# One small load moved from ScalarE's queue to GpSimd's, and one pair of warm-up matmuls taken out, in the start-up of a fused attention and FFN kernel

## The chip, the cores and the metric

The kernel runs on one core of a Trainium2 chip. The metric is the device time of one execution in microseconds (us), lower is better. Times here are of fast runs; row_alone and before_again are single runs, whose state is unknown. The span in a profile is 1.2 to 1.3 us shorter than the device time, since it starts with the first instruction of the program and ends with the last.

TensorE (PE) has two rows in a profile: PE for matmuls and PEld for the loads of their stationary operand. VectorE is DVE, ScalarE is ACT, GpSimd is POOL, and SyncE is SP. SP and ACT issue the transfers (DMAs) here, and in the changed kernel POOL issues one of them.

## The reference

Two branches over the same tokens are mixed by a gate: a linear attention and a SwiGLU FFN.

```python
x = A_x                                               # 1 x 2048 x 640, bf16
g = _sigmoid((x * gate_w).sum(-1, keepdims=True))     # one gate per token
a = _A_ref(x, wqkv, w_phi, wo)                        # 32 heads of 20, softmax feature maps
b = _B_ref(x, w_gate, w_up, w_down)                   # hidden size 1728
return g * a + (1 - g) * b
```

## The kernel before

One long list, `ORDER`, says in which order PE works; loads are issued in front of it in the order of `LOADS`. Only the first few microseconds matter here. There, x comes in 128-token tiles x0 to x3, the v columns of `wqkv` in five row blocks w0 to w4, and the gate vector as a row of 640 numbers, which PE turns into a 641st column beside them. So the gate's dot product comes out of the same matmuls as v.

```python
LOADS = """ x0 w0 x1 w1 x2 w2 x3 w3 w4 f0 h ... """
ORDER = """
H0 ... H9 X0 G H10 H11 H12 U0.0 X1 H13 U1.0 U0.1 X2 U1.1 U2.0 U0.2 ... """

XQ = ["sp", "act", "act", "act"]          # queues of x0..x3
WQ = ["sp", "sp", "sp", "sp", "act"]      # queues of w0..w4
dma("act", gwr[0:5, :], ...gate_w...)     # the gate row, in front of all other ACT loads

def gcol():        # G: turn the gate row, copy it into column 640 of wvg
    ...
    transposes([(o, gwr[0:5, :])], 5)
    copy("dve", wvg[:, :, D:D + 1], o.unsqueeze(2))

def warm():        # H: NWARM = 2 matmuls of constants, their result is not used
    ...
def load_phi():    # h: ACT waits for w3, then loads w_phi
    tr._wait("act", dict([wv_evs[3]]))
    dma("act", wph[:, :, :], ...)
def kv_end():      # N
    for _ in range(NPEW):                 # NPEW = 16
        pe.wait_ge(tr.sem["pe"], 1)       # always met already
```

`X0` turns x0 (five transposes on PE, two copies on DVE), `U0.0` is the first v part (x0 times w0, two matmuls of 320 and 321 columns), `M1` much later needs `w_phi`. The H matmuls keep PE busy while it waits for data.

The softmax here doesn't subtract the row's maximum and nothing guards it: scores larger than these inputs give would overflow.

## Time and profile before

| | before |
|---|---|
| device time, median of 5 runs | 288.73 us (288.59 to 289.27) |
| span in the profile | 287.60 us |
| PE busy | 99% |
| x0, w0, x1 landed | 3.08, 3.89, 4.30 us |
| gate row issued by ACT, landed | 0.82, 2.17 us |
| first v part starts | 4.50 us |
| last matmul at the slow pitch starts | 5.47 us |

The prediction below shows the main lines. One view is added: the timeline of PE alone, just after the start-up. Columns are start, duration, engine, line, operation, what is written and read, shape, and count.

```profile
5.71 0.71 PE L296 MATMUL ps<-wvg,xT 128*128 128x320 bf16 x4
...
6.54 1.53 PE L296 MATMUL ps<-wvg,xT 128*128 128x320 bf16 x10
...
8.19 3.46 PE L296 MATMUL ps<-wvg,xT 128*128 128x320 bf16 x24
11.49 0.38 PE L296 MATMUL ps<-xT,wg 128*128 128x512 bf16 x1
```

Ten matmuls of 320 and 321 columns in 1.53 us is the full pitch, 0.136 us from start to start. Before 5.6 us the same matmul takes 0.267 us. The trace's record of the granted clock begins at 5.61 us, with full clock. Below, "half clock" and "slow pitch" both mean the pitch of 0.267 us for 320 columns (0.107 us for 128, against 0.056 us later). The first FFN matmul (`wg`), at 11.49 us, is a good mark for the end of the start-up.

### The profile page before, as it was taken

How to read it: one execution, taken by the hardware profiler on the slowest of the kernel's cores; microseconds unless marked ns; L12 is line 12 of the kernel's file. 1: busy time of each engine (PE TensorE's matmuls, PEld its weight loads, DVE VectorE, ACT ScalarE, POOL GpSimd, SP SyncE). 2: the span in 40 equal slices, each digit the busy share in tenths (PEclk: the TensorE clock that was granted, in tenths of full speed). 3: DMA queues.
4: the chain of work that ended last, by engine and by line, in shares of the span. 5: the costliest groups of instructions: out<-in, count | busy, mean ns of one | idle time of the engine just before them, and what ended most of it. 6: DMA issues, size and time to landing. Idle time of an engine off the chain costs nothing.

```text
span 287.6 us, 4959 instructions
## 1 busy us (share of the span) xinstructions
PE 284.9 (99%) x1977; PEld 175.2 (61%) x1977; DVE 163.4 (57%) x243; ACT 151.8 (53%) x252; POOL 159.8 (56%) x125
## 2 busy tenths in 40 slices
PE   8999999999999999999999999999999999999997
PEld 7667777675644545557775556675554446656776
DVE  2237748576469978689991465970317899100000
ACT  0767778676775565683535653225576552234112
POOL 8286999879446789836543438350753558501000
PEclk9999999999999999999999999999999999999999
DMA  7979488000010598202393002061020006210101
GB/s 219 190 133 123 100 251 317 5 1 2 2 47 0 114 297 162 51 2 50 65 158 70 5 1 50 2 149 42 2 50 0 3 1 123 52 46 0 49 23 48
DMA packets 48944, 21.62 MB, mean 75 GB/s; under 512 B 39384, under 2 KB 48792, under 8 KB 48920
## 3 DMA queue, kind: packets, MB, share of 16 engines
q1 hardware_dynamic: 47534, 20.59, 32.0%
q10 hardware_dynamic: 1386, 0.71, 0.9%
q8 instruction: 16, 0.26, 0.4%
q14 instruction: 8, 0.07, 0.1%
HBM read 9.29 MB, written 2.62 MB: 41 GB/s over the span
## 4 chain that ended last, share of the span: by engine, by line
PE 99%; DVE 0%; issue 0%
PE ps L296 97%; PE ps L477 1%; PE ps L308 1%; DVE osb L732 0%
## 5 line engine op out<-in xcount | busy, mean ns | idle before, releaser
L324 POOL TENSOR_TENSOR hT<-hT,us 128x512 bf16<-128x512 bf16 (+1 forms) x56 | 65.0, 1173 | 65.3 <-DVE hT L328 47.0
L328 DVE SCALAR_TENSOR_TENSOR hT<-hT,ps 128x512 bf16<-128x512 bf16 (+1 forms) x56 | 37.4, 683 | 66.9 <-ACT hT L314 53.3
L296 PE MATMUL ps<-xT,wg 128*128 128x512 bf16 x260 | 64.6, 379 | 0.0
L296 PE MATMUL ps<-xT,wu 128*128 128x512 bf16 x260 | 64.6, 379 | 0.0
L296 PE MATMUL ps<-wd,hT 128*128 128x320 bf16 (+2 forms) x462 | 63.9, 295 | 0.0
L324 POOL TENSOR_TENSOR ph<-eq,qc 128x1320 bf16<-128x1320 bf16 x16 | 42.3, 2644 | 25.6 <-DVE qc L637 22.2
L296 PEld LDWEIGHTS ps<-wd,hT 128*128 128x128 bf16 x462 | 44.5, 98 | 17.4
L296 PE MATMUL ps<-wqk,xT 128*128 128x320 bf16 x320 | 47.7, 299 | 0.0
L314 ACT ACTIVATE hT<-ps 128x512 bf16<-128x512 f32 (+2 forms) x60 | 35.8, 596 | 16.7 <-PE ps L296 16.5
L296 PEld LDWEIGHTS ps<-xT,wu 128*128 128x128 bf16 x260 | 25.5, 98 | 30.6
L314 ACT ACTIVATE us<-ps 128x512 bf16<-128x512 f32 (+1 forms) x56 | 33.5, 598 | 19.2 <-PE ps L296 18.2
L314 ACT ACTIVATE osb<-ps,omg 128x640 bf16<-128x640 f32 (+2 forms) x17 | 12.9, 757 | 55.8 <-PE ps L296 55.8
L296 PEld LDWEIGHTS ps<-xT,wg 128*128 128x128 bf16 x260 | 25.1, 98 | 27.8 <-ACT oT L314 0.8
L324 POOL TENSOR_TENSOR ekr<-ekr,krec 128x1280 bf16<-128x1280 bf16 x16 | 37.4, 2357 | 5.8 <-DVE krec L338 5.8
L296 PEld LDWEIGHTS ps<-wqk,xT 128*128 128x128 bf16 x320 | 30.5, 98 | 13.1 <-issue 0.4
L314 ACT ACTIVATE eq<-ps 128x640 bf16<-128x640 f32 x32 | 22.3, 703 | 20.9 <-POOL ph L324 10.7
L335 DVE TENSOR_REDUCE ksum<-ekr 128x64 f32<-128x1280 bf16 x16 | 23.5, 1470 | 11.7 <-ACT ekr L314 11.7
L314 ACT ACTIVATE ekr<-ps 128x640 bf16<-128x640 f32 x32 | 22.3, 703 | 8.7 <-PE ps L296 8.2
L335 DVE TENSOR_REDUCE qz<-eq 128x64 f32<-128x1280 bf16 x16 | 23.7, 1478 | 2.6 <-ACT eq L314 2.6
L296 PE MATMUL ps<-wog,oT 128*128 128x320 bf16 (+2 forms) x165 | 24.7, 294 | 0.0
L296 PE MATMUL ps<-wvg,xT 128*128 128x320 bf16 (+1 forms) x160 | 24.6, 301 | 0.0
L335 DVE TENSOR_REDUCE qw<-ez 128x64 f32<-128x1280 bf16 x16 | 23.6, 1476 | 0.0
(73 smaller groups left out, 190.4 us busy)
## 6 DMA issues: line engine op xcount, KB each, us to landing
out_dram<-osb SPq DMA_DIRECT2D x15, 160.0 KB, 1.9
wd<-in_B_w_down_dram SPq DMA_DIRECT2D x1, 2080.0 KB, 10.7
wg<-in_B_w_gate_dram SPq DMA_DIRECT2D x1, 1040.0 KB, 10.1
wu<-in_B_w_up_dram SPq DMA_DIRECT2D x1, 1040.0 KB, 12.2
wg<-in_B_w_gate_dram SPq DMA_DIRECT2D x1, 800.0 KB, 6.2
wu<-in_B_w_up_dram SPq DMA_DIRECT2D x1, 800.0 KB, 7.8
wog<-in_A_wo_dram SPq DMA_DIRECT2D x2, 375.0 KB, 7.2
wvg<-in_A_wqkv_dram SPq DMA_DIRECT2D x4, 160.0 KB, 4.2
```

Of the source, the lines that this page charges most:

```text
L296: last = pe.matmul(o, lhsT=l, rhs=r, start=st, stop=sp_, skip_group_check=sk)
L308: last = pe.transpose(o, i, ident[0:k, 0:k])
L314: return run("act", lambda: act.activation(o, i, func, scale=scale), rd, [o])
L324: return run(e, lambda: eo.tensor_tensor(o, a, b, op), [a, b], [o])
L328: return run("dve", lambda: dve.scalar_tensor_tensor(out=o, in0=a, scalar=s, in1=b, op0=op0, op1=op1), rd, [o])
L335: return run("dve", lambda: dve.tensor_reduce(o, i, AX.X, ALU.add), [i], [o])
L477: last = pe.matmul(bank(2 * pr, 0, P), lhsT=c, rhs=c, start=True, stop=True)
```

## The change

The intent: ACT's queue opens with x1 in place of the small gate row, so x1 comes sooner; GpSimd, which has nothing to load, takes the row. One pair of warm-up matmuls in front of the first v part is dropped. The added waits lie at the end of the k phase.

```diff
-NPEW = 16
+NPEW = 24
@@ ORDER
-H0 ... H9 X0 G H10 H11 H12 U0.0 X1 H13 U1.0 ...
+H0 ... H9 X0 G H10 H11 U0.0 X1 H12 U1.0 ...
@@
-    dma("act", gwr[0:5, :], bass.AP(gate_w.tensor, gate_w.offset, [[P, 5], [1, P]]))
+    dma("pool", gwr[0:5, :], bass.AP(gate_w.tensor, gate_w.offset, [[P, 5], [1, P]]))
```

More of the change, by code (lines that the diff above doesn't have):

```diff
@@ L38 @@
 ORDER = """
-H0 H1 H2 H3 H4 H5 H6 H7 H8 H9 X0 G H10 H11 H12 U0.0 X1 H13 U1.0 U0.1 X2 U1.1 U2.0 U0.2 U1.2 U2.1
+H0 H1 H2 H3 H4 H5 H6 H7 H8 H9 X0 G H10 H11 U0.0 X1 H12 U1.0 U0.1 X2 U1.1 U2.0 U0.2 U1.2 U2.1
 X3 U2.2 U0.3 U1.3 U2.3 U0.4 U1.4 U2.4 V3 Y F0.1 M1 i3 M0 F0.0 M2 V4 M3 M4 K0 K1 I S0 V6 V5 S1 P0
```

## The prediction

> **What bounds the kernel now.** I read the page's busy shares first, then the chain that ended last, then the first 14 us of the timeline, where everything that the change touches lies, and last the DMA landings there.
>
> The busy line and the chain say that this is one long TensorE program:
>
> ```profile
> PE 284.9 (99%) x1977; PEld 175.2 (61%) x1977; DVE 163.4 (57%) x243; ACT 151.8 (53%) x252; POOL 159.8 (56%) x125
> ...
> PE 99%; DVE 0%; issue 0%
> PE ps L296 97%; PE ps L477 1%; PE ps L308 1%; DVE osb L732 0%
> ```
>
> A busy PE is not proof of a full PE, since matmul ends are modelled. I therefore compared the start-to-start times of all matmuls after 5.7 us with columns / 2.4 + 2.5 ns. They fit (0.136 us for 320 columns, 0.216 us for 512) everywhere but at twelve places around the matmuls that read phiT, 0.83 us in all, none touched here. So nothing on VectorE, ScalarE, GpSimd or the queues delays PE from 5.7 us to the end. The end is "when the start-up is over" plus a constant. L477 are the dummy matmuls, L308 the transposes, L296 the real work.
>
> The start-up, from the timeline:
>
> ```profile
> 0.80 0.20 POOL L342 MEMSET ident<- 128x128 bf16 x1 [0.29 <-POOLq L791]
> 0.80 0.40 SPq L350 DMA_DIRECT2D xs<-in_A_x_dram  x1
> ...
> 0.82 0.56 ACTq L350 DMA_DIRECT2D gwr<-in_gate_w_dram  x1
> ...
> 1.24 0.29 POOL L356 TENSOR_SCALAR_AFFINE_SELECT ident<-ident 128x128 bf16<-128x128 bf16 x1 [0.23 <-POOL ident L342]
> ...
> 1.41 1.32 ACTq L350 DMA_DIRECT2D xs<-in_A_x_dram  x3
> ...
> 3.12 0.45 PEld L308 LDWEIGHTS ps<-ident,xs 128*128 128x128 bf16 x5 [0.26 <-DMA xs<-in_A_x_dram]
> ...
> 3.77 0.10 PEld L308 LDWEIGHTS ps<-ident,gwr 5*128 5x128 bf16 x1 [0.20 <-issue]
> ...
> 3.89 0.82 PE L477 MATMUL ps<-const-bfloat16-1.0 128*128 128x128 bf16 x6
> ...
> 4.22 0.17 DVE L320 COPY wvg<-ps 128x5 bf16<-128x5 bf16 x1
> 4.45 0.21 PEld L296 LDWEIGHTS ps<-wvg,xT 128*128 128x128 bf16 x2
> 4.50 0.74 PE L296 MATMUL ps<-wvg,xT 128*128 128x320 bf16 x2
> 4.77 0.74 PEld L308 LDWEIGHTS ps<-ident,xs 128*128 128x128 bf16 x5
> ```
>
> PE waits for x0 (3.12), turns it, turns the gate row (3.77), runs six dummies, then the first v part. That part waits for VectorE's copy of the gate column, which ends at 4.39. Its weight load starts 0.05 us later, and its matmul another 0.05 us later, when the last dummy leaves the array. Only this last 0.05 us is the dummies' doing. The issues in the same stretch are worth a second look:
>
> ```profile
> wvg<-in_A_wqkv_dram SPq DMA_DIRECT2D x4, 160.0 KB, 4.2
> xs<-in_A_x_dram ACTq DMA_DIRECT2D x3, 160.0 KB, 3.9
> ...
> xs<-in_A_x_dram SPq DMA_DIRECT2D x1, 160.0 KB, 2.3
> ```
>
> Adding each issue's landing time to its start: x0 3.08, w0 3.89, x1 4.30, w1 5.50, x2 5.68, w2 6.85, x3 7.05, w3 7.48, w4 7.83 (wN are the row blocks of wvg). PE's weight loads that wait on them start at 3.12, 4.45 (by way of VectorE), 4.77, 5.85, 6.12, 6.95, 7.77, 8.33, 9.16. So x0 has no slack, w2 has 0.10 us, w1 0.35 us, x1 0.47 us. The thing that the change hurries, x1, is not what PE waits for now.
>
> [...] In the trace's packet records the gate row's first packet starts 0.94 us after its ACT issue and it lands 1.35 us after[...]. No GpSimd DMA exists before. [...] from 3.1 to 7.8 us one 160 KB block lands per 0.6 us, whichever queue sent it. [...] Here the pitch of 128-column matmuls is 107 ns until the clock record turns to full at 5.61 us, then 56 ns. [...] Sixteen such blocks are in queue q8, and no PE gap lies near one.
>
> **The change part by part.**
> 1. Two dummies fewer before the first v part: 2 x 0.107 = 0.21 us of cold PE work, of which 0.16 us would only become waiting for VectorE. The matmul can start at 4.45 in place of 4.50: gain 0.05 us. The three-item order after it keeps one dummy pair behind x1. x1's turn, its copies on VectorE and the next v part all follow the first v part, so the 0.05 us is carried.
> 2. The gate row through GpSimd: PE needs it at 3.77 (and loses nothing until about 3.9, as VectorE is busy to 4.22). [...]
> 3. ACT's queue opens with x1 at 0.82 in place of 1.41. Gain by itself: none (slack 0.47). But it crowds others. In the packet records w0's packets follow x0's at about 2.5 us and x1's only begin at 2.98, as if blocks were served in the order of issue. Now x1 stands beside x0 and ahead of w0, and each later x block moves up one place as well. If x0 is slowed, the whole start-up slips. If the places merely swap, x1 lands near 3.9, w0 near 4.3 to 4.4 (need 4.39), w1 near 5.7 (need 5.85), w2 near 7.05 (need 6.95, less what PE gained). The last costs 0.1 to 0.15 us. w3 late by 0.35 us would also put off w_phi, which ACT issues after it, and the M1 matmuls that need it (weight load at 13.43, GpSimd's product done at 13.19): again 0.1 to 0.15 us, but the same delay, not a second one.
> 4. Eight more waits at the end of the k phase. The trace has them two to a record, 106 ns apart: 4 x 0.106 = 0.42 us of PE's sequencer near 75.5 us, while the sequencer is over 1 us ahead of the array (wait for VectorE done at 76.5, matmul at 77.6). Nothing.
>
> Sum for the middle case: -0.05 + 0.12, or +0.07 us: 288.8 us.
>
> **The rivals.** (a) *The hand-over helps*: blocks swap without harm to x0 and w2, only the dummies count: -0.05 us, 288.68. For it: the engines are far from full at 5.2 to 6.4 us in the packet records, so there is room. (b) *x1 slows x0*: if their packets alternate on the 16 engines, x0 lands 0.1 to 0.4 us later. [...] up to +0.3 us: 289.0. For it: the gate row's packets (1.76) came beside x0's (1.84), so two queues are not strictly in line. Against: x1's were not. (c) *The gate row is late*: if GpSimd's path needs over 3.1 us, the column, and with it all, slips by the excess; over 1 us is unlikely. (d) *The clock*: PE idles 0.16 us more before 5.6[...].
>
> **Range and chances.** I give (a) 3 in 10, the swap with a small loss 3 in 10, (b) and (c) together 3 in 10, the rest to (d) and the unknown. The three runs before spread over 0.28 us, so I widen to 288.4 to 289.3. A 2% change is 5.8 us[...]. Within 2%: 0.985.
>
> **What would show it.** Right: the first v part's load still 0.05 us after the gate column's copy; gate row landing before 3.7; x1 landing well before 4.3 and w2 after 6.85; PE without gaps after the start-up; end shifted by just what M1 is shifted. Wrong: x0's turn later than 3.2 (rival b), the gate row's turn waiting for a DMA (c), the 56 ns pitch setting in at a quite different time (d), or a new gap near 77.6 us (the waits do count).

The sum for the middle case: -0.05 us of step 1 and +0.12 us of step 3 make +0.07 us, or 288.8 us; steps 2 and 4 stood in it as nothing. What is cut in step 2 is the reason why it was nothing: the author's sum for the row's landing, which came to 3.1 us and so left 0.6 us to spare, and an estimate of how long GpSimd is held. Rival (b) came to +0.3 us with a term which took 0.1 us off it. The sixteen blocks in queue q8 that the prediction speaks of are instruction packets of 16 KB.

## The result, and the profile after

The changed kernel took 291.32 us (median of 5 runs, 290.48 to 291.76) against 288.73 us. The ratio is 1.0082, with a 95% interval of 1.0062 to 1.0102. A ratio here is the mean time of one kernel's fast runs over that of the other's from the same rounds, so not quite the ratio of the medians. The kernel is slower by 2.4 us by the means and 2.6 us by the medians. That is within 2%, but well outside the predicted range of 288.4 to 289.3 us.

The page's chain of work that ended last now has a transfer in it, which it had not before:

```profile
PE 98%; DMA 1%; issue 0%; DVE 0%; POOLq 0%
PE ps L296 97%; DMA gwr<-in_gate_w_dram 1%; PE ps L308 1%; PE ps L477 0%; DVE osb L732 0%; POOLq L791 0%
```

The timeline of the first microseconds, all engines, shows where:

```profile
0.81 1.37 ACTq L350 DMA_DIRECT2D xs<-in_A_x_dram  x3
...
1.32 0.70 POOL L350 DMA_DIRECT2D gwr<-in_gate_w_dram  x1 [0.80 <-POOLq L791]
2.01 0.23 POOL L342 MEMSET ident<- 128x128 bf16 x1
...
2.48 0.28 POOL L356 TENSOR_SCALAR_AFFINE_SELECT ident<-ident 128x128 bf16<-128x128 bf16 x1 [0.24 <-POOL ident L342]
...
3.58 0.45 PEld L308 LDWEIGHTS ps<-ident,xs 128*128 128x128 bf16 x5 [0.70 <-DMA xs<-in_A_x_dram]
...
4.78 0.10 PEld L308 LDWEIGHTS ps<-ident,gwr 5*128 5x128 bf16 x1 [0.75 <-DMA gwr<-in_gate_w_dram]
...
5.00 0.18 DVE L320 COPY wvg<-ps 128x5 bf16<-128x5 bf16 x1 [0.25 <-PE ps L308]
5.24 0.22 PEld L296 LDWEIGHTS ps<-wvg,xT 128*128 128x128 bf16 x2
```

x0 is turned at 3.58 us in place of 3.12 us, and PE waits for the transfer. Then PE waits again, for the gate row, whose turn moves from 3.77 to 4.78 us. The first v part is 0.80 us later. But this profiled execution is 2.5 us longer, not 0.8. The timeline of PE alone shows the rest:

```profile
6.58 1.28 PE L296 MATMUL ps<-wvg,xT 128*128 128x320 bf16 x4
...
8.19 2.36 PE L296 MATMUL ps<-wvg,xT 128*128 128x320 bf16 x10
...
10.66 3.46 PE L296 MATMUL ps<-wvg,xT 128*128 128x320 bf16 x24
13.96 0.38 PE L296 MATMUL ps<-xT,wg 128*128 128x512 bf16 x1
```

The group of ten takes 2.36 us in place of 1.53 us: PE is still at half clock. The page of this profile has no row for the granted clock, so the pitch must tell. The last matmul at the slow pitch starts at 9.53 us (before: 5.47 us), and the one at 9.79 us is a mixture (0.18 us to the next), which puts the turn at about 9.89 us (estimate). The first `wg` matmul is 2.47 us late, and the whole span is 2.49 us longer. So all of the loss is in the start-up, and nothing after it is slower.

The loss can be added up from the trace. PE idle time in the start-up is what the starts of successive matmuls lie apart beyond columns / 1.2 ns, summed up to the turn of the clock: 0.45 us before, 1.45 us after. (At the slow pitch 320 columns take 0.267 us, which is 1.2 columns per ns.) Work done at half clock takes about twice its time at full clock (0.267 against 0.136 us for 320 columns), so half of the added slow time is lost.

| term | before | after | difference |
|---|---|---|---|
| PE idle in the start-up | 0.45 | 1.45 | +1.00 |
| PE busy at half clock (start to turn, less idle) | 5.61 - 0.85 - 0.45 = 4.32 | 9.89 - 0.85 - 1.45 = 7.59 | half of it is lost: +1.63 |
| two dummies fewer, at full pitch 2 x 0.056 | | | -0.11 |
| sum | | | +2.52 (spans: +2.49) |

### The profile page after: what moved, and what is told of

Read it like the earlier page. It is cut to its first block, busy times and chain, and to the rows that moved or that the text cites. A ratio compares the mean times of both kernels' runs of the same rounds, so it can differ in the third digit from the quotient of the medians.

```text
span 290.1 us, 4959 instructions
## 1 busy us (share of the span) xinstructions
PE 286.4 (99%) x1975; PEld 175.8 (61%) x1975; DVE 163.5 (56%) x243; ACT 151.8 (52%) x252; POOL 160.4 (55%) x126
## 4 chain that ended last, share of the span: by engine, by line
PE 98%; DMA 1%; issue 0%; DVE 0%; POOLq 0%
PE ps L296 97%; DMA gwr<-in_gate_w_dram 1%; PE ps L308 1%; PE ps L477 0%; DVE osb L732 0%; POOLq L791 0%
## 5 line engine op out<-in xcount | busy, mean ns | idle before, releaser
L296 PE MATMUL ps<-wvg,xT 128*128 128x320 bf16 (+1 forms) x160 | 26.0, 313 | 0.0
```

Source lines behind the costliest of these rows:

```text
L296: last = pe.matmul(o, lhsT=l, rhs=r, start=st, stop=sp_, skip_group_check=sk)
```

## The experiments

The theory after reading this: the move of the row does three things. x1, now issued at once, shares the engines with x0 and makes it late. The row itself is late by GpSimd's path. And the idle time that both leave on PE keeps the clock at half for longer. The rivals: the dummies dropped are what lost the clock; the late turn of the clock was chance; the waits alone cost the time. All kernels gave correct results. Times are compared with runs of the kernel before on the same chip. Each kernel was profiled in one execution only, so what a profile shows need not hold for that kernel's other runs.

### queue_only and order_only: one part of the change alone

```diff
# queue_only: the kernel before with
-    dma("act", gwr[0:5, :], ...)
+    dma("pool", gwr[0:5, :], ...)
# order_only: the changed kernel (24 waits, one dummy pair fewer) with
-    dma("pool", gwr[0:5, :], ...)
+    dma("act", gwr[0:5, :], ...)
```

> Only the queue of the gate row is changed; dummies and waits as before. Theory A (the cost is all in the queue move: GpSimd's row lands at about 4.7 us, x1 beside x0 slows x0 to about 3.5 us, PE idles about 1.1 us in that stretch[...]): within 0.6 us of the changed kernel, 290.6 to 291.6 us, gate row turned at about 4.8 us. Theory B (the two dummies fewer are what loses the clock): about 289.2 us, since only the 0.5 us of waiting is left, with the 56 ns pitch setting in before 6.5 us.

> Only the dummy pair and the eight waits are changed; the gate row stays on ScalarE's queue. Theory A: as before or 0.05 us less, 288.6 to 288.9 us, first v part at 4.45 us, clock full near 5.6 us. Theory B (0.16 us more of idle PE is enough[...]): about 290.5 us, pitch of 107 ns until about 9 us.

Measured: queue_only 291.31 us (290.43 to 291.85), ratio 1.0063 (1.0015 to 1.0111). order_only 289.67 us (288.53 to 289.73), ratio 1.0004 (0.9964 to 1.0044). The kernel before in these rounds: 289.05 us (288.52 to 290.86). From the timeline of queue_only:

```profile
3.69 0.45 PEld L308 LDWEIGHTS ps<-ident,xs 128*128 128x128 bf16 x5 [0.82 <-DMA xs<-in_A_x_dram]
...
5.01 0.10 PEld L308 LDWEIGHTS ps<-ident,gwr 5*128 5x128 bf16 x1 [0.86 <-DMA gwr<-in_gate_w_dram]
```

and of order_only:

```profile
4.45 0.47 PE L296 MATMUL ps<-wvg,xT 128*128 128x320 bf16 x2
...
6.78 0.11 PEld L296 LDWEIGHTS ps<-wvg,xT 128*128 128x128 bf16 x2 [1.37 <-DMA wvg<-in_A_wqkv_dram]
```

The queue move alone makes the whole change, with both waits and a slow pitch up to 9.70 us. The dummies alone do what was predicted of them: the first v part starts at 4.45 us, and the clock is full by 4.6 us. order_only's median was above the expected range. Its profile shows another reason for that run: w1 landed at 6.74 us, against 5.50 us in the first profile, and PE waited 1.2 us for it. Whether the other two runs near 289.7 us had the same is not known. Landing times of w0 and w1 vary from run to run in all these kernels (w0 from 3.9 to 4.9 us). The interval of order_only includes 1, so it is not shown to be slower.

### after_filled: the waits kept, PE kept busy

```diff
-H0 ... H9 X0 G H10 H11 U0.0 ...
+H0 ... H9 W5 X0 W6 G H10 H11 U0.0 ...     # Wn: n dummy matmuls
```

> The changed kernel, with five dummies more in front of x0's turn and six in front of the gate row's turn: the waits stay, but PE works through them. Theory A (most of the loss is the clock, held back by PE's idle time): the gate row is still turned at about 4.8 us, but the 56 ns pitch sets in by about 6.5 us, and the time is 289.0 to 289.6 us. Theory C (the loss is the waits themselves and what follows from late data): no change, 291.0 us or more.

Measured: 290.06 us (289.85 to 290.12), ratio 1.0026 (0.999 to 1.0061), so 1.3 us below queue_only. The timeline:

```profile
5.07 0.10 PEld L308 LDWEIGHTS ps<-ident,gwr 5*128 5x128 bf16 x1 [0.20 <-DMA gwr<-in_gate_w_dram]
...
5.53 0.45 PE L296 MATMUL ps<-wvg,xT 128*128 128x320 bf16 x2
```

The row is even later here (5.07 us), but the first v part's two matmuls take 0.45 us, full pitch; the last slow matmul starts at 4.72 us. Eleven useless matmuls made the kernel faster. So the clock is the larger part of the loss. The time is above the 289.0 to 289.6 us expected, because a second wait came out, at `M1`:

```profile
13.31 1.49 POOL L324 TENSOR_TENSOR wbd<-wph,bmask 128x160 bf16<-128x160 bf16 x3 [4.91 <-DMA wph<-in_A_w_phi_dram]
...
14.90 0.79 PE L296 MATMUL ps<-wbd,wT 128*128 128x140 bf16 x12 [0.45 <-POOL wbd L324]
```

w3 landed at 8.25 us in place of 7.48 us, ACT issued `w_phi` behind it, that landed at 13.24 us (before: 11.63), and PE stood 0.61 us. Only 0.8 us of that lateness comes from w3; the rest is `w_phi` itself, which took 5.0 us from its issue in place of 4.1 us. In the changed kernel w3 was as late (8.29 us), but `w_phi` took 3.8 us and PE was later itself, so there is no wait. The span, 1.26 us longer than before, is made up of 0.65 us up to the `wg` mark (12.13 against 11.49 us) and this 0.61 us.

### x1_first_act and decoy_row: which transfer delays which

```diff
# x1_first_act: the kernel before, gate row on ACT, but issued behind x1
-    dma("act", gwr[0:5, :], ...)          # in front of all loads
+        if t == 1: dma("act", gwr[0:5, :], ...)   # in load_x
# decoy_row: the changed kernel, with a load of the same row that nobody reads first on ACT
+    dma("act", gwz[0:5, :], ...)
     dma("pool", gwr[0:5, :], ...)
```

> The kernel before, with the gate row second on ScalarE's queue, behind x1: x1 as early as in the changed kernel, but no GpSimd DMA. If x1 beside x0 is what slows x0: x0's turn at about 3.55 us in place of 3.12 us, the gate row's turn right behind it at about 4.2 us, first v part at about 4.9 us, time 289.1 us when the clock still turns near 5.6 us, up to 291 us when it does not. If x0 was slowed by GpSimd's traffic instead: x0's turn at 3.12 us and 288.7 us.

> The changed kernel, with a second load of the gate row put first on ScalarE's queue, into bytes that nobody reads; PE still uses GpSimd's row. So x1 is issued as late as in the kernel before and only the GpSimd path is left of the queue move. If x1 beside x0 is what slowed x0: x0's turn is back at about 3.12 us, and what is left is the gate row's lateness: its packets start 2 to 2.5 us after GpSimd's issue at 1.3 us, it lands at 4.0 to 4.7 us and PE idles 0.4 to 1.0 us in front of its turn, time between 289.2 and 290.6 us. If GpSimd's DMA slows x0 by itself: x0's turn at 3.5 us again and 291 us.

Measured: x1_first_act 290.35 us (289.83 to 290.88), ratio 1.0037 (0.9999 to 1.0075). decoy_row 290.52 us (289.37 to 291.81), ratio 1.0044 (1.0012 to 1.0077); the kernel before in its rounds 288.99 us (288.64 to 289.88). x0's and the row's turn in x1_first_act:

```profile
3.81 0.45 PEld L308 LDWEIGHTS ps<-ident,xs 128*128 128x128 bf16 x5 [0.94 <-DMA xs<-in_A_x_dram]
...
4.46 0.10 PEld L308 LDWEIGHTS ps<-ident,gwr 5*128 5x128 bf16 x1 [0.20 <-issue]
```

and in decoy_row:

```profile
3.21 0.45 PEld L309 LDWEIGHTS ps<-ident,xs 128*128 128x128 bf16 x5 [0.33 <-DMA xs<-in_A_x_dram]
...
4.62 0.10 PEld L309 LDWEIGHTS ps<-ident,gwr 5*128 5x128 bf16 x1 [0.96 <-DMA gwr<-in_gate_w_dram]
```

The two parts come apart in the profiles. Where x1 is issued at once and GpSimd loads nothing, x0 lands at 3.77 us: x1 beside x0 is what slows x0, by 0.7 us here. Where the decoy holds x1 back to 1.41 us again, x0 lands at 3.17 us, and the row alone, at 4.58 us, keeps PE idle for 0.9 us. In this execution that went with a slow pitch up to 9.36 us. The times are less clean: x1_first_act's interval just includes 1, and decoy_row's four runs split (289.37, 289.93, 291.1 and 291.81 us; the 291.1 us one was profiled), so either delay alone may lose the clock in some executions and not in others.

### row_alone: GpSimd's path without company

```diff
-    dma("pool", gwr[0:5, :], ...)
+    gw_ev = dma("pool", gwr[0:5, :], ...)
+    tr._wait("sp", dict([gw_ev]))
+    tr._wait("act", dict([gw_ev]))
```

> Measures GpSimd's path by itself: the changed kernel, but SP and ScalarE issue no load until the gate row has landed, so nothing shares the transfer engines with it (the time will be some 3 us longer, on purpose). If the row was late through crowding by the x and w blocks: it lands about 2.0 us after GpSimd's issue, at about 3.3 us. If the path itself is that long: it lands at 4.3 us or later, 3 us or more after the issue.

Measured: 293.44 us (one run, slower on purpose). The row, issued at 1.32 us, landed at 3.29 us, 2.0 us after the issue. In the changed kernel it took 3.4 us. The last line of the row's view, in row_alone and then in the changed kernel:

```profile
DMA to landing us min/median/max: 2.0/2.0/2.0
...
DMA to landing us min/median/max: 3.4/3.4/3.4
```

So 1.4 us of it came with the x and w blocks as company: crowding. The other part of the lateness is in the issue: where their first transfer waits for nothing, SP and ACT issue it at 0.80 to 0.82 us, but GpSimd starts on its own at 1.31 to 1.32 us in every profile of these kernels, and is busy with the issue until 2.02 us. What GpSimd does between 0.8 and 1.3 us the profile does not tell.

### before_idle: idle PE time and nothing else

```diff
-H0 H1 H2 H3 H4 H5 H6 H7 H8 H9 X0 G ...
+H0 H1 H2 H3 H4 X0 G ...
```

> The kernel before with ten of its twenty opening dummies removed, so that PE idles about 1.25 us in front of x0's turn while no transfer and no later matmul changes. If idle PE time alone puts the clock off: the 107 ns pitch lasts beyond 6.5 us in the profile and the time rises by 0.5 to 2 us over the kernel before. If the clock only counts time since the first matmul: full clock near 5.6 us, time as before within 0.2 us.

Measured: 289.84 us (289.6 to 290.61), ratio 1.0031 (1.0013 to 1.0049), with ten useless matmuls fewer. From its timeline:

```profile
3.19 0.72 PE L308 MATMUL ps<-ident,xs 128*128 128x128 bf16 x5 [1.12 <-DMA xs<-in_A_x_dram]
...
5.85 1.28 PE L296 MATMUL ps<-wvg,xT 128*128 128x320 bf16 x4
```

The data come as before (x0 at 3.14 us), and the first v part starts at 4.57 us, only 0.06 us later. But the four matmuls at 5.85 us, which took 0.71 us before, take 1.28 us, and the slow pitch lasts to 7.35 us. PE has no new gap after that, so the slow pitch is what the time is lost to. One late turn would not prove the cause, since the turn moves from run to run (before_again, below: about 4.2 us, against 5.6 us in the first profile of the same program). The times do: all four runs are at 289.6 us or more, their interval excludes 1, and nothing but idle time was added.

### before_again and after_again: is the late clock chance?

The kernels are unchanged. The first forecast for before_again: the clock turned at 5.61 us in the first profile, and the time follows at half of any shift of that turn (by the pitches, 0.267 and 0.136 us).

> The kernel before once more, for its profile[...]. [...] (5.61 us in the first profile), and the time follows at half of the shift. If instead the turn is tied to the kernel's start: within 0.2 us of 5.6 us again.

> The changed kernel once more, for its profile and more times. [...] times between 290.3 and 291.9 us. If the late turn of the first profile was chance: a turn before 6.2 us and a time near 289.6 us.

Measured: before_again 288.8 us (one run), after_again 291.2 us (289.4 to 291.46; ratio 1.0035, 0.999 to 1.0081). The kernel before in these rounds: 289.33 us (288.57 to 291.86). The last slow matmul starts at 4.18 us in before_again, against 5.47 us in the first profile of the same program, and at 9.35 us in after_again, against 9.53 us. So the turn moves from run to run, but the changed kernel's lay near 9.5 us both times. The interval of after_again includes 1, so this alone does not show the change to be slower. One of its four runs took only 289.4 us; it was not profiled, so whether its clock turned early is not known. The runs of the kernel before spread over 3.3 us in all, much more than the 0.28 us of the three that the prediction had. Of the 13 runs of the changed kernel and of queue_only, 12 took over 290.4 us; of the 34 comparison runs of the kernel before, 2 did (290.86 and 291.86 us). So, by the times alone, the kernel before seems to fall into the slow start too, but seldom. The 291.86 us run is the only one with a granted clock under 1.0: 0.994, which would be about 3.5 us at half clock (estimate: 0.006 x 290.6 us / 0.5). It was not profiled.

### waits_only: the eight waits

> The kernel before with 24 waits in place of 16 at the end of the k phase, nothing else. If PE's sequencer has over 1 us in hand there: no new PE gap near 77.6 us and the time as before within the spread of its runs. If the waits count: 0.4 us more, with a gap at 77.6 us.

Measured (`NPEW = 24` in the kernel before): 289.26 us (288.92 to 289.42), ratio 1.0005 (0.9988 to 1.0021). After 7 us its matmuls have the same twelve long intervals as the kernel before and no other, so there is no gap near 77.6 us. No cost of the waits is shown.

### gate_first and gate_first_filled: tries at a better kernel

The gate column is needed by the first v part but waits on DVE behind x0's copies. The row lands 0.9 us before x0, so it can be turned first.

```diff
-H0 ... H9 X0 G H10 H11 H12 U0.0 X1 H13 U1.0 ...
+H0 ... H6 G H7 H8 H9 X0 H10 U0.0 X1 W1 U1.0 ...     # gate_first
+H0 ... H6 G H7 H8 H9 X0 W5 U0.0 X1 W2 U1.0 ...      # gate_first_filled
```

> A try at a better kernel, made from the one before: the gate row is turned in front of x0 (it lands at 2.2 us, x0 at 3.1 us), so that the first v part no longer waits for VectorE's gate column behind x0's copies but only for w0 (3.9 to 4.3 us); one dummy pair between x0's turn and it, one dummy behind x1's turn. First v part at 3.95 to 4.4 us in place of 4.50 us. The gain is capped by w1 and w2 (5.5 and 6.85 us in the kernel before): 0.1 to 0.2 us where these land so, 288.5 to 288.6 us; nothing, where w1 lands a microsecond late. [...]

Measured for gate_first: 290.02 us (289.1 to 291.17), ratio 1.0034 (1.0011 to 1.0056). It is slower. In its profile w0 landed at 4.70 us, PE idled 0.93 us in front of the first v part, and the slow pitch lasted to 8.90 us. That was the slowest of its six runs (291.17 us); two others took 289.1 and 289.4 us. With fewer dummies a late w0 leaves PE idle, and the likely cause of the loss is the same trap.

> The second try at a better kernel: the gate row is turned before x0 as in the first try, but five dummies (in place of two) stand in front of the first v part and two behind x1's turn, so that PE has no long idle stretch unless w0 is over 0.5 us late. [...] the loss of the first try (+1.0 us) is gone in most runs; first v part at about 4.2 to 4.4 us, or at w0's landing; 0.1 to 0.2 us less than the kernel before on average, which the spread of both will hide: 288.5 to 289.2 us. If idle PE was not the cause of the first try's loss: 290 us again.

Measured for gate_first_filled: 289.13 us (288.6 to 289.25), ratio 0.9982 (0.9954 to 1.001). In its profile w0 landed at 4.46 us, which is what the first v part waited for (4.60 us), and the last slow matmul starts at 6.10 us. The group of ten matmuls after the start-up, in gate_first and then in gate_first_filled:

```profile
7.57 2.42 PE L296 MATMUL ps<-wvg,xT 128*128 128x320 bf16 x10
...
6.93 1.53 PE L296 MATMUL ps<-wvg,xT 128*128 128x320 bf16 x10
```

The loss of the first try is gone. A gain over the kernel before is not shown, as the interval includes 1. All six runs lie below all four of the changed kernel in the same call (289.25 us at most against 289.4 us at least).

### All profiles side by side

Idle is PE's idle time from the first dummy to the turn of the clock, summed as above; the third column is the start of the last matmul at the slow pitch. row_alone, whose loads were held back on purpose, is left out (idle 3.65 us, last slow matmul at 11.43 us).

| kernel | PE idle in the start-up, us | last slow matmul, us | x0 turned, us | first v part, us |
|---|---|---|---|---|
| before | 0.45 | 5.47 | 3.12 | 4.50 |
| waits_only | 0.52 | 4.15 | 3.19 | 5.04 |
| before_again | 0.55 | 4.18 | 3.23 | 4.84 |
| after_filled | 0.56 | 4.72 | 3.78 | 5.53 |
| order_only | 0.61 | 4.07 | 3.12 | 4.45 |
| gate_first_filled | 0.62 | 6.10 | 3.12 | 4.60 |
| x1_first_act | 1.14 | 6.47 | 3.81 | 5.19 |
| gate_first | 1.17 | 8.90 | 3.12 | 4.83 |
| decoy_row | 1.29 | 9.36 | 3.21 | 5.14 |
| after | 1.45 | 9.53 | 3.58 | 5.30 |
| after_again | 1.55 | 9.35 | 3.49 | 5.40 |
| before_idle | 1.58 | 7.35 | 3.19 | 4.57 |
| queue_only | 1.68 | 9.70 | 3.69 | 5.74 |

With up to 0.62 us of idle time the clock was full soon after 4.1 to 6.1 us; with 1.14 us and more it was slow until 6.5 to 9.7 us. The two groups nearly touch (6.10 and 6.47 us), and within the second the order does not follow the idle time, so the table gives no threshold. Among the six kernels with 0.45 to 0.62 us the last slow matmul lies anywhere from 4.07 to 6.10 us, so something besides the length of the idle time moves the turn; what it is was not measured. That idle time can cost more than the delay it makes is shown by the times: before_idle adds only idle time, starts the first v part 0.06 us later and takes 289.84 us against 288.99 us, after_filled removes mainly that and wins 1.3 us, and gate_first_filled does the same to gate_first. How idle time must lie to hold the clock back is not shown.

## Why the prediction was wrong

**What bounds the kernel** was read rightly. All of the difference lies in the start-up, and PE has no new gap after it.

**Step 1, two dummies fewer: right.** order_only starts the first v part at 4.45 us, as predicted.

**Step 2, the gate row through GpSimd, failed: it was called hidden, and PE waited 0.7 us for it.** The estimate for its landing: 3.1 us. It landed at 4.74 us. Measured, the issue came at 1.32 us, not at 0.8 us as on ACT, and the row took 3.4 us from there in company, 2.0 us in row_alone, so that 1.4 us is crowding. Holding GpSimd did no harm: it was busy with the issue for 0.70 us, and ident was ready at 2.77 us, 0.8 us before x0. So rival (c) came true: counted from 0.8 us the row took 3.9 us in place of the 3.1 us that it could afford, and the first v part was late by that excess, 0.80 us. The row's turn was 1.0 us late.

**Step 3, x1 at the head of ACT's queue, failed in its middle case.** It assumed that blocks merely swap places and x0 keeps its own, from packets that looked as if blocks were served in the order of issue. In the changed kernel x1's packets begin at 2.19 us, among x0's. Rival (b) was the true one: x0 landed 0.45 us later in the changed kernel and 0.69 us later in x1_first_act, above the 0.1 to 0.4 us given. That x1 itself was not waited for held, and so did its earlier landing (3.73 us in place of 4.30 us), which bought nothing. The danger to `w_phi` and `M1` was real too, but hidden by larger delays; after_filled uncovered it, at 0.61 us in place of the 0.1 to 0.15 us predicted, though in part because `w_phi` itself took longer there.

**Step 4, the eight waits: right**, as waits_only shows.

**Rival (d), the clock, was the largest term and was weighed wrongly.** The prediction counted only the 0.16 us of idle time that the dropped dummies leave, and took each rival alone. But (b) and (c) make idle time too: 1.45 us in all in the changed kernel, where the clock turned late. The 0.16 us alone, on top of the 0.45 us that PE idled before, did no harm: order_only had 0.61 us and its last slow matmul at 4.07 us. The size given for (d) is cut, as it was not worked out from a trace; 1.63 us is measured. That holds for one pair of profiles, since the turn in the kernel before came at 5.6 us in one profile and at about 4.2 us in the other. So the turn is at no set time in these runs: it was late where PE idled 1.14 us or more (last slow matmul at 6.47 to 9.70 us, table above), and it moved from run to run.

**Two readings were loose** without bearing on the result: the transfer engines are not "far from full" at 5.2 to 6.4 us (mean busy share 0.92, 257 GB/s against 352 GB/s just before), and one of the twelve long intervals, at 127.5 us, lies 0.5 us from one of the sixteen blocks in queue q8 (instruction packets of 16 KB), at 128.0 us.

**The sum** of the prediction, +0.07 us, thus lacked its two main terms: 1.00 us of new PE idle time and 1.63 us at half clock.

**The range** was drawn from three runs before that happened to lie 0.28 us apart. The later runs of the same kernel spread over 3.3 us.

## What to carry to other kernels

Put what the first instruction waits for alone on the transfer engines: here a second block issued at the same moment from another queue was not free, it made the first 0.4 to 0.7 us late. In a start-up whose clock is not yet full, price idle PE time beyond its length: here about 1.0 us of new idle time cost 2.6 us in the profiled execution, and useless matmuls placed in the waits won half of that back. Add up the idle time of all rivals together before giving each a small chance of its own, and ask for more runs before taking their spread for the noise.

## The start-up's transfers, as measured

- A 1.2 KB row issued by GpSimd landed 2.0 us after the start of its issue in row_alone, and 3.3 to 3.7 us after it beside 160 KB blocks on the other queues.
- In the kernel before, counted from the start of the issue, the first packet came after 0.94 us (gate row, ACT) and 1.03 us (x0, SP); counted from the issue's end, after 0.39 and 0.63 us.
- x0, 160 KB, landed at 3.45 to 3.77 us in the five profiles with x1 issued beside it at the start, and at 3.07 to 3.19 us in the eight with x1 issued 0.6 us later.
- GpSimd's first transfer was issued at 1.31 to 1.32 us in all profiles with one, against 0.80 to 0.82 us for SP and ACT (row_alone, where both were held back, left out).
